# A routed-attention and FFT-gate kernel: one more group's softmax sums go through accumulating DMAs, and thirty warm-up products stand where sixteen did

## The chip, the cores and the metric

The kernel runs on one core of a Trainium2 chip. The core has a matrix engine (TensorE, "PE" in the profile), a vector engine (VectorE, "DVE"), a scalar engine (ScalarE, "ACT"), a general engine (GpSimd, "POOL") and a queue engine (SyncE, "SP") that issues most DMAs. Each takes its instructions strictly in the order in which the program gives them, and they wait for one another on semaphores. The metric is the device time of one execution in microseconds. Three executions of the kernel before took 366.21, 366.43 and 366.46 us; the median is 366.43.

## The reference

Two stages follow each other. The first is attention in which a query sees only the keys of its own cluster; the second is a gated long convolution along the sequence.

```
# attention: q, k, v of 4 batches x 8 heads x 768 positions x 64
q_assign = argmax(normalised q . normalised centroids)      # 16 clusters a head
k_assign = argmax(normalised k . normalised centroids)
scores   = where(q_assign == k_assign, (q @ k.T) / 8, -1e9)
attn     = exp(scores - max) / (sum over keys + 1e-9)
x        = attn @ v                                         # heads put side by side: 4 x 768 x 512
# gate
x1, x2, x3 = split(x @ w_proj)                              # each 768 x 512
x2_conv  = irfft(rfft(x2) * rfft(filter))                   # circular convolution over 768
out      = (x1 * x2_conv * x3) @ w_out
```

## The kernel before

**How the work is cut.** The eight "groups" n = 0 to 7 are half a batch each: four heads, taken as two pairs pr = 0 and 1. For each pair `attention(n, pr)` runs over six blocks of 128 keys (sk = 0 to 5). A block has three score products of 512 columns (L67 or L69 by the array's mode), three exponentials on ScalarE (L647, L650) into one of five buffers `p`, and the products with the values (L661, eight instructions) that add into one pair of PSUM banks. The mask costs no pass of its own: `routing(n)` finds the clusters, and the one-hot rows are written below q and k in the tiles `aug`, so that the score product itself adds a large negative number. `routing` also transposes the loaded q and k of the next groups on TensorE (L551, L562), copies them out of PSUM to `qkP` and casts them into `aug` (L246 on ScalarE, L248 elsewhere). `hyena(b)` is the gate for batch b, after groups 2b and 2b+1; its products (L798, L69) fill TensorE between those of attention.

**The sum of the exponentials.** The denominator of the softmax is a sum over all keys. The blocks are first added to one another into `acc` (two tiles, one for each pr): the first two blocks by three instructions of 512 columns on VectorE or GpSimd (L678, `part`), the other four by one VectorE instruction each (L682). What is left is a sum over the 128 partitions, and it is done in two ways.

- "Late" pairs (groups 0, 1 and 7): `den` multiplies `acc` by a tile of ones on TensorE (L695), `total` copies the result out of PSUM on ScalarE or VectorE (L701, L703), and a small DMA through DRAM (`dd`, 6 KB, L707 and L709) turns it into `dn`. The very last pair (`last`) has a way of its own with more products and no DMA.
- The other pairs (groups 2 to 6): three accumulating DMAs issued by GpSimd (L715) fold the upper half of `acc` on the lower, 64, then 32, then 16 rows; SyncE writes the 16 rows left to DRAM (`dd`, 96 KB, L719) and reads them back so that each partition holds what it must add (`dp`, L721); VectorE adds sixteen rows (`gather`, L725 and L726).

Both then take the reciprocal (L728), send it out and back over all partitions (`dr`, `rb`, L729 and L732), and VectorE multiplies the attention's output with it into `xT` (L761), which `hyena` reads. The same `acc` tile is taken again by the same pr of the next group: its first `part` has to wait until the sum before has been read.

**What sets the order.** `build` first lists every piece of work with the engines that could do it. The constant `ORDER`, a long string, then says the rest: each word is an engine letter and a number (`P1015:3` is piece 1015 on TensorE with PSUM bank 3), in the order in which the pieces are issued. `Plan.follow` reads it. Nothing is scheduled at run time. Which engine casts a tile, which PSUM bank a product takes and how far exponentials run ahead are all fixed there.

**Idle products.** `hot()` fills a tile with ones (L1012) and multiplies it with itself `HOT` times (L1015); nobody reads the results. In the kernel before the tile is the first 640 columns of `y`, into which the filter is loaded later. Of its sixteen products fifteen stand ahead of all other work of TensorE and one among the first transposes.

**The head.** Before the first score product TensorE transposes the first q and k (L562), multiplies them with the centroids (`first_masks`, L497) and VectorE turns that into one-hot rows (L501 to L518), which go into `aug` (L526, L248). GpSimd clears a number of tiles (`constants`), one of them `cbd` (L983).

Of the kernel before, what the change touches and what calls it, by code (L numbers as in the profile page):

```python
# [34 lines left out]
FIRST = 2  # L35
# [4 lines left out]
HOT = 16  # L40
# [84 lines left out]
A35 V0 G18 S45 A46 P14:0 G29 S47 V22 P6:1 G20 S48 P5:2 G28 P11:3 S52 P1:4 G23 P2:5 V36 V53 S51 P16:6 G34 V37 P13:7 V59  # L125
G17 S49 V38 P4:0 V54 A39 A40 P7:1 V60 G19 V55 S50 P10:2 P3:3 G24 V61 P15:4 P9:5 P12:6 G137 V21 V56 P68:7 A66 A63 P70:0
V62 A57 P8:1 G33 S121 V41 A69 P74:2 G27 A58 P76:3 A64 G30 S124 A71 V26 P42:4 A77 V75 G65 S123 G72 P140:5 A67 P142:6
V43 P146:1 V143 S122 P82:7 G25 V141 G32 V44 S120 A73 P80:0 V83 G31 S135 A79 P102:3 V81 G78 P144:2 S134 P138:6 A103 V84
P96:5 A145 G136 S130 P100:4 V85 A97 P94:7 A101 V86 S131 P108:0 A95 G133 V87 A105 S127 P106:3 V88 A139 S126 V89 G104
P149:2 A99 P249:5 S128 G132 P251:4 A151 V93 V91 A250 V90 P243:7 A252 V92 S125 P183:6 V109 P245:5 A244 G98 V107 A184  # L130
S129 P185:0 P187:7 V150 G253 A186 P190:3 S288 V110 P192:6 P194:2 A188 V147 P200:0 V111 S287 A195 P202:7 V112 A246
P204:2 V199 A191 P189:45 V113 A193 V197 A201 A203 V198 P208:3 P210:6 A205 P212:0 V114 P216:7 P196 A211 V207 A209 A213
P218:2 P220:6 A254 P224:3 V148 P226:0 G154 V115 P206 A217 A219 V119 A118 P228:1 V153 P263:7 A116 V155 P214 V117 A221
V215 A248 P293:2 P222 A227 A294 V157 A229 P255:6 V223 A225 P257:0 P295:2 A264 P297:1 P300:3 A258 P261:7 A256 P302:0
V158 P230 A298 V160 A301 A262 V231 A296 P304:6 P310:1 S352 P312:3 A305 P267:72 S291 A303 V156 A232 S292 V159 A311
P233:6 S285 V269 A259 G162 P314:0 V268 S290 P318:1 A313 P299:45 V270 A315 G161 S289 A266 V234 P320:2 S286 P322:7 A319
V271 G152 P163:3 A323 S242 P171:0 A260 P164:6 S235 V272 P326:1 V273 G307 P328:7 A165 P306 A327 V166 A167 G358 P330:1
V274 A169 P316 G353 A331 V275 G309 A329 P334:3 P172:1 A321 V168 S278 P336:7 A175 G356 P177:2 V276 S280 V170 P324 A335
G308 S277 A173 V176 S279 V174 P419:361 S236 G247 A337 A181 V317 G357 A265 P338:0 P178:7 S453 A339 P332 S454 A421 V420
A422 V325 P359:0 A179 P361:1 P363:3 P340 A362 A360 V182 G426 A364 P366:6 V237 P368:1 A342 V180 P370:0 S238 G355 P376:3  # L140
P378:7 A371 V333 P365:45 S282 G354 A369 S455 A367 P380:2 A379 S283 P384:0 V374 P386:1 A381 P388:6 S281 P392:7 V341
A377 P372 S284 A387 S239 A385 P394:2 A389 S240 V375 P396:3 P343:1 A397 V373 A395 P427:063 V383 A393 A344 S345 P400:2
P402:7 A429 P404:1 V391 P382 A430 A428 A401 P461:0 A405 V399 P463:3 P465:6 A403 P390 A466 S346 A425 V407 P468:2
P435:17 S456 A464 V241 P470:6 P472:3 P398 A471 V437 A462 G476 V436 A473 P478:6 V438 P480:0 P482:1 P486:7 A481 P488:3
V347 P406 V439 A469 S348 A433 S458 V440 A483 P409:0 S418 V441 G475 A408 S459 P490:2 A489 P494:1 P467:45 V442 S460 A495
A487 S349 V443 G477 A410 P474 A479 A491 S446 V444 P496:3 S411 V485 P498:1 P502:7 A497 P701:062 S448 A434 S445 A424
V431 S447 P484 A499 V493 S350 S452 P504:3 P506:1 S457 P492 A505 V423 A704 S412 V501 A503 S520 P500 A507 S449 A703 S451
P639:3 V509 P508 A640 S738 A702 P641:7 V413 P643:1 A510 G708 P511:3 S414 A642 G432 P646:0 A644 V512 P648:2 P650:6 A647
G706 P656:7 S513 P658:1 A649 P660:3 P645:45 S450 V351 A657 A661 V653 A651 S416 P664:0 P666:2 A659 P668:7 V655 S415
P672:3 P674:6 A669 P676:1 V707 P652 A673 S514 V654 A677 A665 V663 P709:731 A675 A667 P680:0 V671 P682:6 S741 P684:2  # L150
A681 P662 A685 A711 V515 A683 V679 P743:0 S516 P670 A710 S740 A744 A712 S735 P745:2 V417 P747:6 P750:0 P752:1 P717:37
V687 A753 A746 S518 A748 S517 P754:1 A714 V718 P760:2 G689 P678 S736 V719 A755 G758 V720 S700 A751 P686 V721 P762:6
P764:3 A688 V722 P768:7 P770:1 P772:0 A761 V723 G757 P749:45 A765 A769 V724 P776:2 A771 P778:3 P780:7 P756 A779 V759
A763 V519 A705 G690 P766 V725 A781 V726 P521:1 S728 V767 S804 P523:3 A522 S729 A777 P531:6 S727 V525 A773 S732 V524
P526:7 A532 S730 V775 G691 P784:1 S739 P786:2 P528:0 A787 S742 A527 P533:3 A713 S734 V529 P788:6 P564:2 S733 V534 A789
S737 P774 V535 A785 G537 A715 V530 S692 A565 P805:7 V536 P807:6 P809:1 P812:3 A808 V539 P814:0 P816:2 A810 P782 V783
A806 A815 P822:6 A817 P824:1 P826:7 V538 A823 P830:0 P790 A813 V791 A831 A827 P540:2 S866 A792 P543:6 G819 V542 S693
P867:307 A825 V541 S731 V544 G821 P811:45 A869 V545 A870 V546 G793 A868 P548:1 V547 A873 P832:2 P834:6 V549 G716
P551:0 A833 P838:3 V550 P818 A835 G820 V552 A839 V553 P840:7 P842:2 V829 P875:163 A843 P556:0 V554 A877 S906 P828 A841
V837 A876 G794 A878 P846:2 P566:7 A847 V557 G555 P848:1 P850:3 V694 P909:6 P559:2 A910 P836 V695 V560 A851 S696 A871  # L160
V558 S903 G562 P911:6 V567 P568:3 S907 A912 V561 P913:0 P883:76 A569 G795 V845 S908 A879 S904 A849 P570:2 A914 S698
V884 G563 V885 P916:3 P918:1 P579:0 V886 A919 P920:6 P926:7 A580 P928:1 V887 A917 P844 A921 V853 A929 S796 P572:03
A927 P852 A573 V888 G855 V574 P930:6 G872 V575 P934:1 P581:7 A931 V889 A854 G576 S797 P936:0 P583:3 V582 A882 S901
P938:6 V890 P915:45 A584 A937 V891 G923 A939 P942:7 P922 A880 V571 S896 V577 A943 S894 V925 A874 P587:30 S697 V892
P585:6 V578 G856 S895 A588 A935 P932 S893 V586 G924 A881 S902 V589 V590 P944:2 S899 P946:7 V798 P950:1 P952:6 A947
S905 P594:0 V933 P596:3 A595 A951 P940 A953 V799 V941 S800 G857 A945 P954:7 S970 P1089:0 P598:1 A955 S898 A1090 V699
P1091:6 P1093:2 P1096:7 P1098:0 P948 V949 A1099 A1092 S801 A1097 P1100:0 S802 P1106:6 A1094 P956 V957 S858 A1107 A1101
P1108:7 P600:2 A958 V592 G959 P1110:6 V591 A1109 P1114:0 P1095:45 A599 G593 A1111 V601 V597 S859 P1116:7 P1118:1
P1151:623 A1117 G1105 A1115 A1119 P609:7 A1152 V1154 S1186 P602:01 A1153 V1103 S1187 P1159:236 V1104 A603 S897 A1158
V605 G1155 S900 V604 P1102 A1161 V1113 G960 S1191 A1162 S1190 A1160 P1122:0 P1124:1 A1123 P1167:23 S1192 V803 A610  # L170
G607 P1126:6 V1168 P1112 A1127 G606 V860 A1125 V1169 A1156 P1130:0 G961 P1132:7 V861 V1170 P1134:6 S862 A1131 P1193:1
P1195:2 P1197:3 P1120 A1196 V1121 A1135 A1198 P1200:0 A1133 P1202:2 V1171 P1204:6 P1210:3 A1194 P1212:7 P1128 A1203
S864 V1172 A1201 S1188 V1129 A1211 P611:1 S962 A1163 P1214:2 S863 P1218:0 A1166 P1220:3 V612 P1136 S1185 V1173 A1213
A1205 V1137 P1222:1 A1215 P613:7 A1138 P617:62 S963 A1221 P1199:45 V608 A618 S1189 A614 V1174 P1226:3 P1228:7 P1206
A1227 V620 G1208 A1223 V1175 A1219 P1230:3 V619 A1229 P1216 G1139 S1178 V1176 A1231 G622 S1177 A1157 V964 P1234:1
S1183 P615:0 A1164 V965 G621 P1224 S966 V616 S1180 V1207 S1179 P1236:2 V1209 P1232 A1237 V865 A1235 A1165 P1238:6 V623
P1325:730 S967 A1239 V1217 S968 G1140 P1317:216 S1150 A1328 S1182 A1326 V1225 A1327 S1254 P1240 A1320 S1184 A1319
S1181 A1318 P1255:0 V1233 P1257:3 P1259:7 A1256 P626:1 A1260 A1258 P624:2 P1262:6 V969 G1141 P631:0 A625 A627 V1241
P1264:7 P629:3 A1265 A1263 P981:2 V630 G1243 P971:1 V1321 P973:7 G1324 A972 S1142 A982 P983:6 G1323 V975 A1242 S628
V974 P976:3 A632 V984 P978:1 A977 V985 P1266:2 P1272:7 V979 P1014:0 A1267 S1143 V980 P1274:3 P1276:6 S1352 V987  # L180
P1280:2 A1275 P1261:45 G1244 A1273 V986 S1358 A1281 V988 A1015 S1356 P1282:1 P1284:3 V989 P990:7 A1283 S1351 P1288:2
# [47 lines left out]
def build(T):  # L229
# [25 lines left out]
    def ap(h):  # L255
        return bank(h.ids[0])
# [359 lines left out]
    def attention(n, pr, sins):  # L616
# [8 lines left out]
        for sk in range(NT):  # L625
# [568 lines left out]
```

## Time and profile before

| | us |
|---|---|
| median of three executions | 366.43 |
| the profiled execution | 366.52 |
| its span, first to last instruction | 364.7 |
| TensorE busy in it | 353.9 (97%) |
| VectorE busy | 339.3 (93%) |
| ScalarE busy | 271.1 (74%) |
| GpSimd busy | 137.1 (38%) |
| first score product starts at | 18.35 |
| first product of hyena(0) starts at | 107.19 |

The profile is of one execution. "Busy" is the time in which an engine had at least one instruction under way. The view of groups has a line for each place in the code and shape, with how often it ran, its total time and its mean in nanoseconds; behind the second bar stands the idle time before it and who ended that. The view of the chain follows the work that ended last back to the start: each row has a start, a length and what it was. The timeline lists instructions in order of time, and its brackets hold the idle time before a row and what ended it. The view of stretches gives the busy time of each engine in a window, the granted clock of TensorE as a share of full speed, and the DMA engines' share and rate.

### The profile page before, as it was taken

What the parts mean: (1) busy time and instruction counts of PE and PEld (TensorE: products, weight loads), DVE (VectorE), ACT (ScalarE), POOL (GpSimd) and SP (SyncE); (2) the same over time, 40 slices, a digit from 0 to 9 for tenths busy, and PEclk for the clock granted to TensorE, in tenths of its full rate; (3) what the DMA queues carried; (4) which work ended last, traced back from release to release, by engine and by line L of the source; (5) the groups of instructions that cost most, each with busy time, mean ns of one, the idle gap of its engine ahead of it and who ended that gap; (6) DMA issues with size and microseconds to landing.
All of it is one profiled execution on the core that took longest, in us unless ns stands there. A gap on an engine that the chain in (4) does not pass through costs nothing.

```text
span 364.7 us, 8483 instructions
## 1 busy us (share of the span) xinstructions
PE 353.9 (97%) x3254; PEld 198.8 (55%) x3254; DVE 339.3 (93%) x470; ACT 271.1 (74%) x502; POOL 137.1 (38%) x167
## 2 busy tenths in 40 slices
PE   8799999999999999999999999999999999999994
PEld 4445445454555555665565555555655556475771
DVE  8899889998999999989987999999999999999992
ACT  5999989789878777898987667789969826532232
POOL 8930841122131644344143463432340363045500
PEclk9999999999999999999999999999999999999998
DMA  9990999165576568678667948375755640410214
GB/s 171 226 248 14 218 180 179 26 166 132 120 134 147 102 108 129 130 148 151 131 125 193 174 111 155 43 156 56 178 80 155 89 61 17 162 43 2 117 59 173
DMA packets 88004, 45.69 MB, mean 125 GB/s; under 512 B 76488, under 2 KB 82012, under 8 KB 87964
## 3 DMA queue, kind: packets, MB, share of 16 engines
q1 hardware_dynamic: 84076, 35.16, 40.9%
q0 software_dynamic: 2960, 9.77, 18.6%
q8 instruction: 25, 0.41, 0.5%
q10 hardware_dynamic: 928, 0.23, 0.3%
q14 instruction: 15, 0.12, 0.1%
HBM read 31.59 MB, written 7.40 MB: 107 GB/s over the span
## 4 chain that ended last, share of the span: by engine, by line
PE 77%; DVE 9%; ACT 8%; DMA 3%; issue 2%; SPq 0%; DVEq 0%
PE bank L69 33%; PE pair L661 26%; PE bank L798 6%; PE bank L551 4%; ACT p L650 3%; DVE acc L682 3%; PE bank L583 2%; DMA dn<-dd 2%; PE bank L1015 2%; ACT aug L246 2%; ACT p L647 2%; PE bank L67 2%; DMA aug<-ohT 1%; PE bank L695 1%; PE bank L470 1%
## 5 line engine op out<-in xcount | busy, mean ns | idle before, releaser
L661 PE MATMUL pair<-p,vraw 128*64 128x385 f32 x768 | 140.4, 488 | 0.0
L650 ACT ACTIVATE p<-bank 128x512 f32<-128x512 f32 x192 | 108.5, 614 | 18.0 <-PE bank L69 15.6
L682 DVE TENSOR_TENSOR acc<-p,acc 128x1536 f32<-128x1536 f32 x64 | 112.1, 1751 | 2.1
L661 PEld LDWEIGHTS pair<-p,vraw 128*64 128x64 f32 x768 | 54.5, 136 | 47.6 <-issue 38.8
L69 PE MATMUL bank<-aug,aug 80*64 80x256 bf16 (+3 forms) x708 | 78.9, 327 | 1.3 <-DMA aug<-ohT 0.7
L647 ACT ACTIVATE p<-bank 128x512 f32<-128x512 f32 x96 | 57.8, 613 | 16.8 <-PE bank L69 11.3
L69 PEld LDWEIGHTS <-aug 80*64 80x64 bf16 (+1 forms) x708 | 40.9, 109 | 42.4 <-issue 29.7
L715 POOL DMA_DIRECT2D acc<-acc x30 | 24.1, 805 | 75.1 <-DMA acc<-acc 30.6
L678 POOL TENSOR_TENSOR acc<-p,p 128x512 f32<-128x512 f32 x23 | 29.8, 1298 | 48.6 <-ACT p L650 13.6
L69 PE MATMUL bank<-xT,wpj 128*64 128x384 bf16 x480 | 46.3, 326 | 0.0
L69 PEld LDWEIGHTS <-wpj 128*64 128x64 bf16 x480 | 27.6, 110 | 15.8 <-issue 5.3
L246 ACT CAST aug<-qkP 64x768 bf16<-64x768 f32 x43 | 35.4, 829 | 0.7
L246 ACT COPY qkP<-bank 128x512 f32<-128x512 f32 (+1 forms) x56 | 28.4, 562 | 7.9 <-PE bank L69 5.8
L69 PEld LDWEIGHTS <-y 128*64 128x64 bf16 x480 | 23.8, 110 | 11.5 <-issue 2.4
L822 DVE TENSOR_TENSOR tm<-bank,hm 128x512 f32<-128x512 f32 x44 | 27.9, 682 | 0.9 <-POOL y L826 0.2
L826 POOL TENSOR_TENSOR y<-tm 128x512 bf16<-128x512 f32 x17 | 21.5, 1275 | 13.9 <-DVE tm L822 8.7
L69 PE MATMUL bank<-wout,y 128*64 128x512 bf16 x192 | 23.1, 379 | 0.0
L798 PE MATMUL bank<-wpj,xT 128*64 128x512 bf16 x192 | 21.9, 379 | 0.0
L248 POOL CAST aug<-qkP 64x768 bf16<-64x768 f32 x17 | 13.9, 827 | 20.5 <-DVE dn L728 8.3
L246 ACT COPY ob<-bank 128x512 f32<-128x512 f32 x21 | 12.2, 594 | 11.0 <-PE bank L69 9.3
L900 POOL TENSOR_TENSOR y<-yy,x 128x768 bf16<-128x768 f32 x7 | 13.1, 1868 | 18.7 <-DVE yy L897 13.8
L551 PE MATMUL bank<-ident,qkraw 128*128 128x128 f32 x144 | 18.1, 276 | 0.0
(161 smaller groups left out, 447.2 us busy)
## 6 DMA issues: line engine op xcount, KB each, us to landing
qkraw<-in_k_dram SPq DMA_DIRECT2D x32, 192.0 KB
vraw<-in_v_dram SPq DMA_DIRECT2D x16, 384.0 KB
qkraw<-in_q_dram SPq DMA_DIRECT2D x31, 192.0 KB
rb<-dr SPq DMA_DIRECT2D x30, 192.0 KB
out_dram<-ob SPq DMA_DIRECT2D x11, 512.0 KB
acc<-acc POOLq DMA_DIRECT2D x10, 384.0 KB, 5.0
acc<-acc POOLq DMA_DIRECT2D x10, 192.0 KB, 3.9
wpj<-in_moe_w_proj_dram POOLq DMA_DIRECT2D x4, 384.0 KB, 6.3
```

What stands on the lines that cost most here:

```text
L69: T.nc.tensor.matmul(out[64 * i:64 * i + 64], lhsT[:, 64 * i:64 * i + 64], rhs, start=start, stop=stop)
L246: T.nc.scalar.copy(out, in_)
L551: T.nc.tensor.transpose(bank(h.ids[i // 4])[:, block(i % 4, 2 < i < NT)], raw(ss[i // NT], i % NT), T.ident)
L647: T.nc.scalar.activation(o, ap(h).rearrange("p (a b) -> p a b", a=2), Act.Exp, scale=0.125)
L650: T.nc.scalar.activation(flat(s)[:, lo:lo + 512], ap(h), Act.Exp, scale=0.125)
L661: T.nc.tensor.matmul(o[64 * hp:64 * hp + 64, ch, :385], T.vraw[vs][:, hp, sk * D:(sk + 1) * D], T.p[slots[sk]][:, hp, 384 * ch:384 * ch + ...
L678: alu(e).tensor_tensor(o, x, y, op=Alu.add)
L682: T.nc.vector.tensor_tensor(T.acc[os], T.p[slots[sk]][:, :, :S], T.acc[os], op=Alu.add)
L715: op(("POOL", .8), lambda e, rows=rows: T.nc.gpsimd.dma_start(flat_()[:rows], flat_()[rows:2 * rows], accum_op=Alu.add), te, r=[], w=AK, b ...
L798: T.nc.tensor.matmul(ap(h)[64 * i:64 * i + 64], T.xT[xs][:, kt, tokens(m, i, w_)], T.wpj[:, kt, DM:2 * DM], start=kt == 0, stop=kt == ND - 1)
L822: op(("DVE", .68), lambda e, i=i, cs=cs, r=r, h=h: T.nc.vector.tensor_tensor(T.tm[r][:, cs], ap(h), hmrow(i, (0, 2, 2, 3)[2 * r + cs]), op ...
L826: op({"POOL": 1.3, "DVE": .68}, lambda e, i=i, r=r: alu(e).tensor_tensor(T.y[:, i, r], T.tm[r][:, 0], T.tm[r][:, 1], op=Alu.add if r else ...
```

## The change

`FIRST` goes from 2 to 1, so that the two pairs of group 1 leave the "late" way and take the accumulating DMAs; `LATE = 14` and `spread` say for the last group what was said before in other words (pairs 14 and 15 are group 7, and `spread` holds for the last pair alone, as `last` did). `HOT` goes from 16 to 30, and the products get a tile of their own, 512 columns wide, of which the first 128 serve as weights. `ORDER` is another string throughout.

In the new order twenty idle products stand ahead of all other work of TensorE, eight more among the transposes and centroid products before the first score product, and two behind it. Beside the pieces that the first paragraph names, some pieces stay what they are and change their engine: of the 48 `part` instructions 33 run on VectorE where 25 did, and 15 on GpSimd where 23 did; ScalarE gets three more casts to `aug` (46 for 43), two more copies to `qkP` and two loads of q and k to issue, and gives three copies of the output to VectorE. The first product of hyena(0) stood in TensorE's order between the value products of group 2's two pairs; it now stands behind the first score product of group 3's second pair. One load of `w_proj` now stands in GpSimd's queue behind the third accumulating DMA of group 2's first pair. In the head GpSimd clears `cbd` as one of its first pieces, where it did so behind other clears and a cast.

```diff
-FIRST = 2
+FIRST, LATE = 1, 14
-HOT = 16
+HOT = 30
...
 ORDER = """
-A35 V0 G18 S45 A46 P14:0 G29 S47 V22 P6:1 G20 S48 P5:2 G28 P11:3 S52 P1:4 G23 P2:5 V36 V53 S51 P16:6 G34 V37 P13:7 V59
...
-        late = n == NG - 1 or n < FIRST
+        late = n < FIRST or 2 * n + pr >= LATE
+        spread = last and late
         if late:
             h, den_, dk = Bank(), lambda: T.den, ["den"]
...
-        if not last:
+        if not spread:
             if late:
...
     def hot():
-        op(("DVE", .6), lambda e: T.nc.vector.memset(T.y[:].rearrange("p i r d -> p (i r d)")[:, :640], 1.0), 0, w=["hot"])
+        op(("DVE", .5), lambda e: T.nc.vector.memset(T.hot, 1.0), 0, w=["hot"])
         for i in range(HOT):
             h = Bank("head")
             op(("PE", .215), lambda e, h=h: T.nc.tensor.matmul(
-                ap(h), T.y[:].rearrange("p i r d -> p (i r d)")[:, 512:640], T.y[:, 0, 0], start=True, stop=True), .1 * i,
+                ap(h), T.hot[:, :128], T.hot, start=True, stop=True), .1 * i,
                r=["hot"], w=[h], alloc=h, free=[h])
...
+    T.hot = tl([128, 512], BF16, "hot")
```

More of the change, by code (lines that the diff above doesn't have):

```diff
@@ L130 @@
[L130 to L139, printed above, removed]
@@ new lines @@
+S876 V611 P1132:2 S1204 P629:3 A1133 V621 P1120 A1174 G1176 S1205 V623 A1129 S1203 V622 A899 P1134:2 P1136:0 V628
+P1140:1 P1142:6 A1137 V821 P1130 A1141 A1143 V624 P1177:701 A1135 V630 V1122 A1173 V1123 P1144:6 P1138 G978 A1179
+S1208 V1121 A1145 V1131 S1168 A1180 P1148:3 S1209 P1150:2 P1152:6 P1146 A1151 S877 V1139 A1153 A1178 P1211:2 A1149
+P1213:6 P1215:0 P1218:1 A1184 S1207 P1185:73 V1147 A1212 G979 A1219 P631:2 A1214 V1186 G625 A1216 V1187 P1220:1
+P1222:6 P1228:0 A1221 V1188 G1181 P1230:3 P1232:7 P1236:1 P1154 A1233 V1189 A1223 A1237 V1155 P1238:7 P1240:6 A1156
@@ L226 @@
+V1926 P1950:0 V1931 P1946:1 P1947 P1951 P1932:4 V1948 P1933 V1952 S1949 P1936 P1939:7 A1934 S1953 A1937 P1940 P1942:3
+V1941 S1938 P1943 V1944 S1945
 """
@@ L759, in attention @@
         xv = lambda: T.xT[xs][:, kt].rearrange("p (a b) -> p a b", a=2)
-        for a_ in [slice(0, 2)] if not last else [slice(0, 1), slice(1, 2)]:
-            op(("DVE", .6 if last else 1.01), lambda e, a_=a_: T.nc.vector.scalar_tensor_tensor(
-                xv()[:, a_], osv()[:, a_], eps(), ap(rk[a_.start])[:, :384].unsqueeze(1) if last else rbv(), op0=Alu.add,
-                op1=Alu.mult), te + (4 if last else 12), r=[("osb", o3)] + (rk[a_] if last else rk), w=[("xT", xs, kt)],
-               free=rk[a_] if last else [], lock=True)
+        for a_ in [slice(0, 2)] if not spread else [slice(0, 1), slice(1, 2)]:
+            op(("DVE", .6 if spread else 1.01), lambda e, a_=a_: T.nc.vector.scalar_tensor_tensor(
+                xv()[:, a_], osv()[:, a_], eps(), ap(rk[a_.start])[:, :384].unsqueeze(1) if spread else rbv(), op0=Alu.add,
+                op1=Alu.mult), te + (4 if spread else 12), r=[("osb", o3)] + (rk[a_] if spread else rk), w=[("xT", xs, kt)],
+               free=rk[a_] if spread else [], lock=True)
     INV = [("inv", j) for j in range(4)] + [("inv", j, i) for j in (4, 5) for i in range(2)]
```

185 lines of the change are left out of this document (95 added, 90 removed).

## The prediction

> **What bounds the kernel now.** I read the stretches first, then the chain, then the groups. The page gives one busy line for the span:
>
> ```profile
> span 364.7 us, 8483 instructions
> PE 353.9 (97%) x3254; PEld 198.8 (55%) x3254; DVE 339.3 (93%) x470; ACT 271.1 (74%) x502; POOL 137.1 (38%) x167
> ```
>
> An average of 97% and 93% leaves open which of the two is the bound. The stretches say it (window, length, then PE, PEld, DVE, ACT, POOL with counts, granted clock, DMA share, GB/s):
>
> ```profile
> 0.00:20.00 20.00, 16.40 (x108) 8.65 (x109) 17.03 (x47) 15.82 (x31) 17.62 (x49) 1.00 1.01 199
> 20.00:60.00 40.00, 39.02 (x296) 19.35 (x294) 37.27 (x49) 38.36 (x71) 15.34 (x23) 1.00 0.80 160
> 60.00:120.00 60.00, 59.90 (x500) 30.47 (x500) 57.30 (x60) 51.16 (x97) 12.55 (x12) 1.00 0.54 125
> 120.00:200.00 80.00, 79.91 (x738) 46.31 (x736) 74.89 (x98) 65.83 (x120) 33.92 (x34) 1.00 0.72 138
> 200.00:320.00 120.00, 119.35 (x1137) 67.50 (x1134) 116.62 (x157) 86.62 (x162) 43.62 (x40) 1.00 0.57 111
> 320.00:357.00 37.00, 37.00 (x472) 25.52 (x471) 34.82 (x62) 11.15 (x23) 14.09 (x10) 1.00 0.13 50
> ```
>
> From 60 us on TensorE is idle for 0.10, 0.09, 0.65 and 0 us: there the length is the sum of its instructions, and what is added to or taken from them counts in full. VectorE has 2.73 + 2.70 + 5.11 + 3.38 + 2.18 = 16.1 us of slack after 20 us, thinly spread. From 20 to 60 us three engines are nearly full together: ScalarE has 40 - 38.36 = 1.64 us left, TensorE 0.98. Ahead of 20 us it is a matter of waits. These are the rows of the head and of VectorE in it:
>
> ```profile
> 1.58 5.68 PE L1015 MATMUL bank<-y 128*128 128x512 bf16 x13 [1.58 <-DVE y L1012]
> 1.58 6.11 PE L1015 MATMUL bank<-y 128*128 128x512 bf16 x15 [1.58 <-DVE y L1012]
> 7.54 0.82 PE L562 MATMUL bank<-ident,qkraw 128*128 128x128 f32 x6
> 9.17 0.67 PE L397 MATMUL bank<-identb,fw 128*128 128x128 bf16 x4
> 10.01 1.84 PE L497 MATMUL bank<-qkP,cb 128*32 128x384 f32 x16
> 14.57 1.62 PE L497 MATMUL bank<-qkP,cb 128*32 128x384 f32 x16 [1.03 <-ACT qkP L246]
> 18.35 0.38 PE L67 MATMUL bank<-aug,aug 80*128 80x512 bf16 x1 [0.79 <-DVE aug L248]
> 11.35 0.22 DVE L324 COPY cbd<-bank 64x64 f32<-64x64 f32 x1 [1.05 <-POOL cbd L983]
> 11.83 1.05 DVE L501 STREAM_TRANSPOSE sim<-bank 128x384 f32<-128x384 f32 x2
> ```
>
> Thirteen idle products take 5.68 us (about 0.43 each), the next two add 0.43 together, 0.22 each. The rate doubles at about 7.1 us, and nothing later falls back: every stretch reads a clock of 1.00, though TensorE stood still for 1.03 and 0.79 us.
>
> **Part 1, group 1's sums leave TensorE.** The chain of waits holds the products that go, one row for each pair (start, length):
>
> ```profile
> 72.57 0.78 PE bank L695 x8
> 85.05 0.78 PE bank L695 x8
> ```
>
> They stand where TensorE has no idle time, so two of them are worth -1.56 us. What a pair takes instead, and the neighbours of it, by the groups and the DMA issues:
>
> ```profile
> L701 ACT ACTIVATE den<-bank 128x384 f32<-128x384 f32 x4 | 2.0, 498 | 2.0 <-PE bank L695 2.0
> L725 DVE TENSOR_REDUCE dn<-dp 128x12 f32<-128x192 f32 x10 | 4.8, 482 | 0.0
> L726 DVE TENSOR_SCALAR dn<-dn 128x12 f32<-128x12 f32 x10 | 3.4, 339 | 0.3
> L715 POOL DMA_DIRECT2D acc<-acc x30 | 24.1, 805 | 75.1 <-DMA acc<-acc 30.6
> acc<-acc POOLq DMA_DIRECT2D x10, 384.0 KB, 5.0
> acc<-acc POOLq DMA_DIRECT2D x10, 192.0 KB, 3.9
> acc<-acc POOLq DMA_DIRECT2D x10, 96.0 KB, 3.7
> ```
>
> For two pairs: VectorE +2 x (0.48 + 0.34) = +1.6 us; GpSimd +6 issues x 0.8 = +4.8 us, beside 62% idle time; ScalarE one copy of `den` less (-0.50). SyncE loses two writes and two reads of 6 KB and gets two writes and two reads of 96 KB. In its queue the write for pair (1,0) waits for the third fold, and three mask writes for pair (2,1) stand behind it; by my count of the work ahead these are wanted some 10 us later, so I cost them at nothing; if that cover is gone, each microsecond of it goes to the first score of (2,1).
>
> The sum's consumer has to wait longer. Pair (3,1) shows the new way:
>
> ```profile
> 159.54 0.82 POOL L715 DMA_DIRECT2D acc<-acc  x1 [7.00 <-DVE acc L682]
> 182.72 0.49 DVE L725 TENSOR_REDUCE dn<-dp 128x12 f32<-128x192 f32 x1
> 193.72 1.01 DVE L761 SCALAR_TENSOR_TENSOR xT<-osb,rb 128x768 bf16<-128x768 f32 x1
> 82.99 1.76 DVE L682 TENSOR_TENSOR acc<-p,acc 128x1536 f32<-128x1536 f32 x1
> 105.55 1.00 DVE L761 SCALAR_TENSOR_TENSOR xT<-osb,rb 128x768 bf16<-128x768 f32 x1
> 107.19 3.62 PE L798 MATMUL bank<-wpj,xT 128*64 128x512 bf16 x32
> ```
>
> From the first fold to the first of the folded sum's instructions on VectorE it is 182.72 - 159.54 = 23.2 us, and 34.2 us to the product with `rb`. With a den product the same distance was 105.55 - 84.75 = 20.8 us (from the end of the pair's last addition, 82.99 + 1.76). So the first product of `hyena(0)`, which began 1.6 us behind that row, cannot stand at 107 any more: 34 us behind 84.75 and the same 1.6 give about 120, and the changed order puts it there, behind the first score product of group 3's second pair. No instruction is added by that, but between the two pairs of group 2 TensorE now has attention alone to do, and so has no filler when an exponential is late. From the durations of the pieces I count 12.75 us of VectorE against 12.09 us of TensorE for that pair, so VectorE sets the pace there by 0.66 us, less what runs ahead. I take +0.4 us, with 0 and +0.66 as bounds.
>
> **Part 2, sums of two blocks move to VectorE.** The rows of both engines, and those of ScalarE that part 3 uses:
>
> ```profile
> L678 DVE TENSOR_TENSOR acc<-p,p 128x512 f32<-128x512 f32 x25 | 17.3, 717 | 0.2 <-ACT p L650 0.2
> L678 POOL TENSOR_TENSOR acc<-p,p 128x512 f32<-128x512 f32 x23 | 29.8, 1298 | 48.6 <-ACT p L650 13.6
> L650 ACT ACTIVATE p<-bank 128x512 f32<-128x512 f32 x192 | 108.5, 614 | 18.0 <-PE bank L69 15.6
> L246 ACT CAST aug<-qkP 64x768 bf16<-64x768 f32 x43 | 35.4, 829 | 0.7
> L246 ACT COPY qkP<-bank 128x512 f32<-128x512 f32 x34 | 18.3, 604 | 1.6 <-PE bank L551 1.5
> L442 ACT ACTIVATE tm<-bank,hw 128x512 f32<-128x512 f32 x7 | 4.8, 699 | 1.4 <-DVE hm L446 1.4
> ```
>
> Eight `part` instructions cost VectorE 8 x 17.3/25 = +5.5 us and save GpSimd 8 x 1.3 = 10.4 us that nobody lacks. The remaining changes of side (three output copies come, some copies, casts and gate products go) cancel to within a microsecond or two. With part 1 VectorE gets some 5 to 7 us more, against 16.1 us of slack. Bounds: 0 if the slack lies where the work comes, 7 if it doesn't. I put nothing on it beyond the 0.4 above, since the slack is over twice the load in every long stretch; the upper end is a rival below.
>
> **Part 3, ScalarE early.** By the two orders, ScalarE has up to the end of group 1's first pair three casts more (3 x 0.83), a copy to `qkP` (0.60) and an exponential (0.61), and less by a copy of mask rows (0.83, as long as a cast) and one `den` (0.50): +2.4 us, and it issues two loads more, for which I add 0.3 in all: 2.7. It has 1.64 us idle between 20 and 60 us. If all of this is usable, 1.1 us remain; if ScalarE's waits for VectorE's filter products (1.4 of the 1.64, L442 in that stretch) stay as they are, 2.4 remain; and if TensorE or VectorE hold the end of the stretch anyway, nothing. I take +1.5, between the first two and nearer the first, because any shift opens some of those waits; bounds 0 and 2.7.
>
> **Part 4, fourteen more idle products.** Five more ahead of the transposes: at the rate behind 7.1 us 5 x 0.216 = 1.08 us, less 0.1 for the shorter clearing of the tile, so the first transposes start at about 8.5 in place of 7.54. Eight lie among pieces with waits of 1.03 and 0.79 us and cost 8 x 0.216 = 1.7 us at most. Against this stands `cbd`: VectorE waited 1.05 us for it at 11.35, and that wait goes. The first eight centroid products took half of 1.84 us from 10.01 on, so their result stood at about 10.95 and `sim` at 11.83 had 0.9 us of slack, made by `cbd`. The delay of 0.98 eats this slack and 0.1 more; four more of the filter's transposes (L397, 0.17 each, and L400, under 0.1 each) stand ahead of the centroid products, some 0.3 beyond what `fw` made TensorE wait for. So the first score product comes 0.4 us later, at 18.75; bounds -0.8 (the slack all gained) and +1.5 (nothing of it). The two idle products behind the first score, 0.43 us, stand where ScalarE's exponentials lead the chain: I take half, 0.2; bounds 0 and 0.43.
>
> The granted clock is 1.00 from 7.1 us on, through gaps of 1.03 us. The Trainium skill, "TensorE: Matmul & The Clock Gate", Part 1 ("The HAM clock gate"), says that the clock is held at half until the array was busy for a window of about 3.4 us, counted in time and not in products, and that it falls back after an idle window of that length. The trace agrees as to the start (the rate doubles after 5.5 us of products), and the gaps here are under a third of such a window, so by this rule the products placed in gaps protect nothing that the profile shows; where they would, the sum would gain what is priced as the last rival below.
>
> **The sum.** -1.56 (den products) + 0.4 (no filler in group 2) + 1.5 (ScalarE early) + 0.4 (head) + 0.2 (idle products behind the score) = +0.94 us. The profiled execution took 366.52 us, 1.8 of it around its span, and is 0.09 above the median of 366.43. 366.52 + 0.94 = 367.46; against the median 367.4.
>
> **Rivals.**
> - Faster. The order is another one throughout, and each of my positive terms is a wait that it may cover: with ScalarE's 2.7 hidden and the filler not missed, -1.56 + 0.2 + 0.4 = -1.0 gives 365.4; with the head's slack gained as well (-0.8 in place of +0.4), 364.3. For it: every product that goes stood in a full stretch. Against: 20 to 60 us is full on three engines, and what is added lies there.
> - VectorE becomes the bound behind group 1: then its 5 us stand in place of the 0.4 and hide ScalarE's. -1.56 + 0.6 + 5 = +4.0, 370.4; with 5.4 instead 370.8. It decides where VectorE's idle time in 60 to 120 us (2.70) is used up. Against: TensorE's own idle time there is 0.10.
> - The `acc` tile comes free too late. The tile of pair (1,1) can be taken by pair (2,1) only when the third fold was read:
>
> ```profile
> 100.09 1.29 POOL L678 TENSOR_TENSOR acc<-p,p 128x512 f32<-128x512 f32 x1
> 178.28 0.37 SPq L721 DMA_DIRECT2D dp<-dd  x1
> ```
>
> By these rows the first sum of (2,1) stood 100.09 - 84.75 = 15.3 us behind the last addition of (1,1), and a folded pair holds its tile for up to 178.28 - 159.54 = 18.7 us from the first fold. 3.3 us of wait, passed on by five buffers `p` that fill: less the den products and with the head, 366.4 - 1.56 + 0.6 + 3.3 = 368.8. It decides if fold and write take over 15 us; two folds of 5.0 and 3.9 us and a third of 3.7 leave them at 13 when GpSimd isn't late.
> - No change: the -1.56 is eaten by waits just so, 366.4.
> - The idle products save a clock that falls in executions without a profile: a fall between 14 and 19 us would cost up to 2 us. Three times within 0.25 us of each other speak against; I count it with "faster", for 0.02.
>
> **How the numbers follow.** A measurement of this kernel can tell about 0.2%, 0.73 us, from no change. My forecast (366.7 to 368.6, by the bounds of its own terms) gets 0.42, of which 0.06 lies within 0.73; VectorE as bound 0.08; the late tile 0.08; faster 0.32; no change 0.10. Slower: 0.36 + 0.08 + 0.08 = 0.52; same 0.06 + 0.10 = 0.16; faster 0.32. The range goes from the fastest of "faster", 364.3, to the upper price of VectorE, 370.8; outside it lie combinations of late tile and full VectorE, and gains of which I see no source.
>
> **What would show it.** Right: no L695 for two pairs, TensorE still idle under 0.3 us between 60 and 120 us; ScalarE's share of 20 to 60 us up to 39 us or more, and the end of group 1's first pair about 1 to 2 us later; first score product at about 18.7; the first product of `hyena(0)` near 120. Wrong on ScalarE: the first value products of group 1 at the same time as before. Late tile: a wait of (2,1)'s first `part` for the write of `dd`, and TensorE idle near 100 us. VectorE: TensorE idle by several microseconds in short waits for `p` behind 75 us. The forecast fails on the other side if the first score product comes before 18 us.

## The result and the profile after

The changed kernel takes 370.79 us (median of six executions, 368.95 to 372.11), the kernel before 366.36 (six beside it). The ratio is 1.0114, with a 95% interval of 1.0096 to 1.0132: the change makes the kernel slower by 4.4 us. The time lies in the predicted range (364.3 to 370.8) by its last hundredth; the forecast was 367.4. The executions also scatter more than those of before, over 3.2 us in place of 0.4 (over 1.4 in nineteen later executions of the kernel before).

The profiled execution took 369.83 us, about 1 us less than the median, with a span of 368.0. Its stretches (window, length, PE, PEld, DVE, ACT, POOL with counts, clock, DMA share, GB/s) and the first row of its list of TensorE's waits:

```profile
20.00:60.00 40.00, 38.36 (x285) 19.01 (x285) 37.77 (x48) 38.36 (x73) 17.53 (x23) 1.00 0.83 166
60.00:120.00 60.00, 57.65 (x465) 30.27 (x463) 56.68 (x61) 53.56 (x99) 14.51 (x17) 1.00 0.75 140
120.00:200.00 80.00, 78.38 (x734) 46.71 (x732) 76.90 (x102) 59.60 (x111) 32.52 (x31) 1.00 0.69 131
200.00:320.00 120.00, 120.00 (x1125) 70.16 (x1123) 115.59 (x156) 89.35 (x164) 42.60 (x39) 1.00 0.60 121
...
PE bank L69 <- DMA aug<-ohT: 4.2, 3, 2.0
```

TensorE's idle time between 60 and 120 us rose from 0.10 to 2.35 us, and between 120 and 200 us from 0.09 to 1.62. Its waits for the DMAs that write the mask rows into `aug` rose from 0.7 us to 4.2: 0.89 us at the first score product of group 1, 2.02 at that of group 3, 1.31 at the second of group 5. VectorE is no fuller than before between 60 and 120 us (56.68 against 57.30 us). The longest of the three, in the timelines of TensorE, SyncE and GpSimd, and GpSimd's loads of `w_proj` in the list of DMA issues (count, size, us to landing):

```profile
111.04 1.46 PE L662 MATMUL pair<-p,vraw 128*64 128x385 f32 x8
114.53 1.06 PE L69 MATMUL bank<-aug,aug 80*64 80x512 bf16 x10 [2.02 <-DMA aug<-ohT]
...
104.89 1.44 SPq L723 DMA_DIRECT2D dp<-dd  x1
106.42 4.04 SPq L483 DMA_DIRECT2D aug<-ohT  x4
...
108.31 0.76 POOL L717 DMA_DIRECT2D acc<-acc  x1 [3.79 <-DMA acc<-acc]
108.81 0.83 POOL L1007 DMA_DIRECT2D wpj<-in_moe_w_proj_dram  x1
...
wpj<-in_moe_w_proj_dram POOLq DMA_DIRECT2D x4, 384.0 KB, 6.0
```

The four writes for pair (3,0) leave SyncE by 110.46 us and are waited for until 114.53. In the middle of them GpSimd issues a quarter of `w_proj`, which takes about 6 us to land. The kernel before issued all four quarters by 56 us. Its own rows for (3,0) left no earlier: the last of the four writes is the fourth of the first row here, and the second row begins with the first score product of group 3.

```profile
108.81 2.44 SPq L482 DMA_DIRECT2D aug<-ohT  x4
114.97 1.48 PE L69 MATMUL bank<-aug,aug 80*64 80x512 bf16 x16
```

That write left at 111.25 us, and TensorE came to the product at 114.97 without a wait. In the changed kernel TensorE was there at 114.53 - 2.02 = 112.51 us, since products of `hyena(0)` no longer stand in front. The head, with ScalarE's first exponential of both kernels (the first row is of the kernel before):

```profile
18.80 0.63 ACT L650 ACTIVATE p<-bank 128x512 f32<-128x512 f32 x1
```

```profile
1.46 7.25 PE L1017 MATMUL bank<-hot 128*128 128x512 bf16 x20 [1.46 <-DVE hot L1014]
8.55 0.82 PE L563 MATMUL bank<-ident,qkraw 128*128 128x128 f32 x6
18.87 0.38 PE L67 MATMUL bank<-aug,aug 80*128 80x512 bf16 x1
20.25 0.64 ACT L651 ACTIVATE p<-bank 128x512 f32<-128x512 f32 x1
```

The first score product comes 0.52 us later, the first exponential 1.45 us.

### The profile page after: what moved, and what is told of

Its sections match the earlier page's. It is cut to its first block, busy times and chain, and to the rows that moved or that the text cites. A ratio compares the mean times of both kernels' runs of the same rounds, so it can differ in the third digit from the quotient of the medians.

```text
span 368.0 us, 8530 instructions
## 1 busy us (share of the span) xinstructions
PE 355.2 (96%) x3253; PEld 205.9 (56%) x3256; DVE 344.6 (94%) x479; ACT 271.8 (74%) x504; POOL 134.3 (36%) x164
## 4 chain that ended last, share of the span: by engine, by line
PE 72%; DVE 11%; DMA 8%; ACT 5%; issue 2%; SPq 1%; POOL 0%; DVEq 0%; POOLq 0%; ACTq 0%
PE bank L69 32%; PE pair L662 23%; PE bank L800 6%; DVE acc L683 4%; DMA aug<-ohT 3%; DMA acc<-acc 3%; PE bank L552 2%; PE bank L1017 2%; PE bank L584 2%; PE bank L67 2%; DMA dp<-dd 1%; ACT qkP L247 1%; DVE acc L679 1%; ACT p L651 1%; PE bank L471 1%
## 5 line engine op out<-in xcount | busy, mean ns | idle before, releaser
L69 PE MATMUL bank<-aug,aug 80*64 80x512 bf16 (+3 forms) x692 | 77.9, 327 | 5.1 <-DMA aug<-ohT 4.2
L717 POOL DMA_DIRECT2D acc<-acc x36 | 28.7, 797 | 104.6 <-DMA acc<-acc 47.4
L69 PE MATMUL bank<-xT,wpj 128*64 128x384 bf16 x496 | 48.0, 326 | 0.2 <-ACT p L648 0.2
L247 ACT CAST aug<-qkP 64x768 bf16<-64x768 f32 x46 | 37.9, 830 | 1.9 <-PE bank L69 1.1
L69 PEld LDWEIGHTS <-wpj 128*64 128x64 bf16 x496 | 30.9, 110 | 14.4 <-issue 5.6
L247 ACT COPY qkP<-bank 128x512 f32<-128x512 f32 (+1 forms) x59 | 30.3, 563 | 8.4 <-PE bank L69 5.9
L69 PEld LDWEIGHTS <-y 128*64 128x64 bf16 x496 | 26.0, 110 | 10.9 <-issue 2.5
L679 POOL TENSOR_TENSOR acc<-p,p 128x512 f32<-128x512 f32 x15 | 19.2, 1278 | 24.1 <-ACT p L648 11.5
L679 DVE TENSOR_TENSOR acc<-p,p 128x512 f32<-128x512 f32 x33 | 21.7, 689 | 1.5 <-DMA dd<-acc 1.1
L552 PEld LDWEIGHTS bank<-ident,qkraw 128*128 128x128 f32 x144 | 15.5, 141 | 4.7 <-ACT p L651 1.9
```

The costliest lines, as they stand in the source:

```text
L69: T.nc.tensor.matmul(out[64 * i:64 * i + 64], lhsT[:, 64 * i:64 * i + 64], rhs, start=start, stop=stop)
L247: T.nc.scalar.copy(out, in_)
L552: T.nc.tensor.transpose(bank(h.ids[i // 4])[:, block(i % 4, 2 < i < NT)], raw(ss[i // NT], i % NT), T.ident)
L679: alu(e).tensor_tensor(o, x, y, op=Alu.add)
L717: op(("POOL", .8), lambda e, rows=rows: T.nc.gpsimd.dma_start(flat_()[:rows], flat_()[rows:2 * rows], accum_op=Alu.add), te, r=[], w=AK, b ...
```

## The experiments

The first theory was that TensorE loses its time to mask rows that land late, because of where SyncE and VectorE have them in their queues. The rivals were VectorE as the bound, the idle products, and the accumulating DMAs as such. Times are to be held against 370.8 (changed) and 366.4 (before).

**1. Nobody waits for the rows.**

```diff
+UNREAD = [(3, 0), (5, 0)]
...
+                        T.junk[64 - 64 * hp + 16 * j:80 - 64 * hp + 16 * j] if (n, pr) in UNREAD else
                         T.augs[a][hp][j][64 - 64 * hp:80 - 64 * hp], T.ohT[rows]), due + .3 * hp,
```

> The changed kernel, but the eight mask writes for the first pairs of groups 3 and 5 go to a tile that nobody reads, so their score products do not wait for these rows (they use the rows of an earlier group: the mask of those two pairs is not this group's). VectorE, the DMAs and every queue do what they did. Theory 'mask rows': TensorE loses its 2.3 us ahead of group 3 and 1.5 us ahead of group 5 to nothing but these writes landing late; without them 3.8 us go: from 370.8 to about 367.0, and the spread between executions (369 to 372) shrinks to under 1 us, since the time to landing is what varies. Rival 'VectorE is the bound': the wait only moves, TensorE then waits for exponentials or sums behind it: less than 1 us gained, 370 or more. Rival 'idle products': no change.

Measured 367.05 us (ten executions, 364.94 to 370.08): 3.7 us gone with all of VectorE's work and all DMAs in place. VectorE isn't the bound; the waits are the loss. In its profile TensorE still waits 1.7 us for other mask rows (0.78 at group 1, 0.92 at 122.36 us). The spread did not shrink, so something else varies as well.

**2. The rows leave earlier, by order alone.**

```diff
-... V743 ... V775 S531 ... V776 ... V777 ... V744 ... S748 ... S746 ... S747 ... S745 ...
+... V743 V744 ... V775 ... V776 ... V777 ... S748 ... S746 ... S747 ... S745 S531 ...
-... S882 S881 S1196 S1198 S1195 S1197 ...
+... S1196 S1198 S1195 S1197 S882 S881 ...
```

(V744 and its like are L609; S531 reads `dp`, S745 to S748 and S1195 to S1198 write mask rows, S881 and S882 write `rb`.)

> The changed kernel with words of the order moved and no work changed: on VectorE the last one-hot instruction (L609) of groups 1, 3 and 5 stands right behind the transpose L607 (in group 3 it stood behind three sums of 1.85 us together, in group 5 behind 2.1 us of other work); on SyncE the read of dp for pair (1,1) stands behind the four mask writes for (3,0), and the two rb writes behind those for (5,0). Theory 'mask rows', with the place in the queues as the cause: the rows of group 3 land 1.1 to 1.8 us earlier, those of group 5 1.5 us or more, TensorE's waits fall from 4.2 us to 1.5 or less: 367.8 to 369. Rival 'VectorE is the bound': it does the same work, so within 0.5 us of 370.8. Rival 'idle products': no change.

Measured 370.76 us: no gain. The waits ahead of groups 3 and 5 were gone, but others stood in their place. One was again for mask rows, directly ahead of the first product of `hyena(0)`, where the second pair of group 3 begins. Behind the moved `rb`, `xT` came late, then a copy of `ob` on VectorE, and TensorE stood still for 1.81 us:

```profile
122.73 0.63 PE L69 MATMUL bank<-aug,aug 80*64 80x512 bf16 x6 [1.56 <-DMA aug<-ohT]
...
203.01 0.62 PE L69 MATMUL bank<-aug,aug 128*64 128x512 bf16 x4 [1.81 <-DVE ob L249]
203.44 2.33 PE L662 MATMUL pair<-p,vraw 128*64 128x385 f32 x8
```

The stretches around the second show what happened next (granted clock third from the right):

```profile
202.00:203.00 1.00, 0.00 (x0) 0.00 (x0) 1.00 (x3) 0.52 (x1) 0.09 (x1) 1.00 1.00 331
203.00:204.00 1.00, 0.99 (x8) 0.64 (x9) 1.00 (x2) 0.55 (x2) 0.73 (x1) 0.97 1.00 385
204.00:205.00 1.00, 1.00 (x6) 0.43 (x4) 1.00 (x3) 1.00 (x3) 0.00 (x0) 0.50 1.42 293
205.00:206.00 1.00, 1.00 (x8) 0.40 (x6) 0.90 (x3) 0.02 (x1) 0.00 (x0) 0.50 0.92 164
206.00:207.00 1.00, 1.00 (x8) 0.61 (x6) 1.00 (x1) 0.00 (x0) 0.00 (x0) 0.50 0.97 168
207.00:208.00 1.00, 1.00 (x13) 0.65 (x11) 0.55 (x1) 0.49 (x2) 0.00 (x0) 0.82 1.26 90
```

The clock went to half for about 3.4 us, by my estimate at a cost of some 1.7 us: the wait was paid twice. The products bear the clock out: eight value products took 2.33 us, where the same eight took 1.46 in the changed kernel's timeline.

**3. The same without moving `rb`.** The `rb` writes stay; two mask writes of (3,1) go ahead of the read of `dp` as well.

```diff
-... V743 ... V775 S531 ... V776 ... V777 ... V744 ... S748 ... S745 ... S534 ... S751 ... S752 ...
+... V743 V744 ... V775 ... V776 ... V777 ... S748 ... S745 S751 S752 S531 ... S534 ...
```

> The changed kernel with the order mended without the two rb writes being moved: L609 behind L607 in groups 1, 3 and 5 on VectorE; on SyncE the four mask writes of (3,0) and two of (3,1) ahead of the read of dp for pair (1,1). In the run before, the waits for the mask rows ahead of groups 3 and 5 were gone, but TensorE waited 1.81 us at 201 us for a copy of ob on VectorE, which stood behind xT and so behind the rb writes that had been moved back, and behind that wait its granted clock was 0.58 for 4 us. Theory 'mask rows': without that new wait 2 to 3.5 us go: 367.3 to 368.8. Rival 'VectorE is the bound': another wait takes the place again, 370 or more.

Measured 371.24 us, and a new wait again, in the lists of TensorE's waits and in VectorE's and SyncE's timelines:

```profile
PE pair L662 <- ACT osb L686: 3.3, 1, 3.3
...
116.24 0.48 DVE L727 TENSOR_REDUCE dn<-dp 128x12 f32<-128x192 f32 x1 [5.58 <-DMA dp<-dd]
...
109.56 0.58 SPq L723 DMA_DIRECT2D dp<-dd  x1
```

Now the read of `dp` was the one that left at 109.6 to 110.1 us, and VectorE's wait for it ended at 116.24, 6.7 us after the issue began; the median of such reads in this run's list of DMA issues, counted the same way, is 4.0. VectorE stood behind it for 5.58 us, the copy to `osb` behind VectorE, TensorE behind the copy. In the changed kernel it was the mask rows; here it was `dp`: whatever SyncE issues at that time lands late. Both show in the same window, and that is where the load of `w_proj` runs.

**4. Without the idle products, in the changed and in the mended order.** The fourteen additional products are not issued; the second run has the order of experiment 3 in addition.

```diff
+SKIP = {1, 2, 3, 5, 10, 16, 18, 19, 22, 23, 24, 25, 26, 29}
-            op(("PE", .215), lambda e, h=h: T.nc.tensor.matmul(
+            op(("PE", .215), lambda e, h=h, i=i: None if i in SKIP else T.nc.tensor.matmul(
```

> The changed kernel with the fourteen additional idle products not issued: fifteen stand ahead of the transposes and one among them, as before. Theory 'mask rows': the head alone changes; transposes start 1.1 us earlier, the first score product 0.5 to 1.0 us earlier, all behind it moves along, but the waits ahead of groups 3 and 5 stay: 369.8 to 370.4. Rival 'idle products': they are what made the kernel slower: 14 x 0.216 = 3.0 us go, 367.8. If they hold up the clock in executions without a profile, it becomes slower than 371.

> The same order as the run above and, in addition, without the fourteen additional idle products. If the waits for mask rows and the idle products ahead of the head are separate losses, both go: 1.4 to 1.7 us for the head from what the run above gives, 365.6 to 367.0, and it is at or under the kernel before (366.4). If they are two names of one loss (a later head that only shifts into a wait), no better than the better of the two alone, 367.4.

Measured 367.46 us (366.31 to 370.53) and 370.03 us. The head of the first:

```profile
7.17 0.82 PE L564 MATMUL bank<-ident,qkraw 128*128 128x128 f32 x6
17.12 0.38 PE L68 MATMUL bank<-aug,aug 80*128 80x512 bf16 x1
18.85 0.64 ACT L652 ACTIVATE p<-bank 128x512 f32<-128x512 f32 x1
```

The five products in front cost 8.55 - 7.17 = 1.38 us, and the first exponential moves by 20.25 - 18.85 = 1.40: nothing behind them absorbs any of it. That is more than the 1.08 us of five products at the full rate; the rest, 0.3 us, is by my estimate from the two starts that in the changed kernel's profile one to two products more ran at 0.43 us before the rate doubled. The remaining gain of the median is not the head's: in the profiles the wait ahead of group 3 stayed (2.32 us), and the one in group 5 (1.31 us) was not there. The second run has the same wait for `osb` as experiment 3, 3.4 us.

**5. Idle products in the wait itself.**

```diff
-SKIP = {1, 2, 3, 5, 10, 16, 18, 19, 22, 23, 24, 25, 26, 29}
+SKIP = {24, 25, 26, 29}
-... S751 P823:0 ...
+... S751 P2:1 P3:3 P4:1 P6:3 P11:1 P17:3 P19:1 P20:3 P23:1 P24:3 P823:0 ...
```

> The changed kernel without the additional idle products in the head, ten of them placed instead directly ahead of the first score product of group 3, where TensorE waits 2.3 us for mask rows (10 x 0.216 = 2.2 us, so they end about when the rows land). Its twin without them gave 367.46 (366.31 to 370.53 in ten executions), the slow ones with a lower mean granted clock (0.993 and 0.994). Theory 'a wait of about 2 us lets the clock fall in some executions': TensorE is busy in the wait, the clock stays, no execution over 368, median 366.5 to 367.2. Rival 'the spread is that of the landing of the rows alone': same median and spread as the twin, or up to 0.5 us more where the rows land early.

Measured 368.09 us (eight executions, 367.64 to 370.77), not under its twin's 367.46. None of them had a mean clock under 0.997, where three of the twin's ten had 0.993 or 0.994 and took 369.2 to 370.5. That fits products that hold the clock, but does not show it: none in eight against three in ten can be chance, and the kernel before has an execution with 0.995 that took 366.25 us. What it shows is that executions of over 370 us occur with a clock of 0.998 and 1.000 too, so the clock isn't the whole of the spread. That the landing of the rows is the rest is not shown; none of the long executions was profiled.

**6. Group 1's sums back on TensorE, with and without the idle products.**

```diff
-        late = n < FIRST or 2 * n + pr >= LATE
+        late = n <= FIRST or 2 * n + pr >= LATE
...
-... G423 ... P420 A441 ... G424 ... G527 ... P678:6 ... G528
+... P423:0 P420 A441 A424 ... P678:6 P527:7 V528 ...
```

> The changed kernel with the sums of group 1 taken back to TensorE: eight den products for each of its two pairs, copies of den, small DMAs; no accumulating DMAs for them; everything else stays in its place in the queues (the later first product of hyena(0) too). Theory 'mask rows': TensorE gets 1.56 us more; VectorE is freed of two gathers (1.5 us) and of 1.1 us of waiting for the acc tile, SyncE of the long reads of dp, so the rows of group 3 land about 1.8 us earlier: 370 to 371. Rival 'the accumulating DMAs themselves are the loss': back to the time of before and 1 us of slack: under 368.5. Rival 'den products were pure cost': 372.3.

> The changed kernel with both named parts undone: group 1's sums on TensorE again, and no additional idle products. What is left is the new order with its moved pieces. If the parts add up, 368.6 less 1.4 to 3.3 us: 365.3 to 367.2. If the new order by itself is worse than that of before, over 367.2.

Measured 368.61 and 368.50 us. By the first the accumulating DMAs look like a loss of 2.2 us; by the second, with both named parts undone, the order alone is still 2.1 us behind the kernel before. In the profile of the first TensorE waits for no mask rows behind 60 us; in that of the second (370.36) two waits of 1.33 us each stood at 124 and 197 us. The parts do not add up: without the idle products it is 367.46 us, without the fold 368.61, without both 368.50.

**7. The load of `w_proj` alone.** One word of the order moves.

```diff
-... G387 A393 ... A807 G369 V532 ...
+... G387 G369 A393 ... A807 V532 ...
```

> The changed kernel with one word moved: the load of the second quarter of w_proj, which GpSimd issues at 108.8 us in the changed order (all four were issued by 56 us before), goes to 61 us, into GpSimd's idle time. The prediction did not price it. Theory 'the load meets the mask rows': the four writes for (3,0) were issued by 110.5 us and landed at 114.5, 4.1 us later, where those for (5,0) took 2.6; without the load they land 1.0 to 1.7 us earlier and TensorE's 2.3 us ahead of group 3 shrink by as much, and where the wait stays under 2 us the clock does not fall in other executions either: 368.3 to 369.8. Rival 'SyncE's queue and VectorE alone set the landing': no change, 370.3 to 371.3.

Measured 367.24 us (ten executions, 366.38 to 367.45; ratio to before 1.0016, 1.0007 to 1.0025). One DMA issued at 61.3 in place of 108.8 us takes 3.5 us off, where 2.5 was expected at best, and the spread falls from 3.2 to 1.1 us. Between the two profiles the gain is 2.4 us; the rest is in executions that were not profiled. The changed kernel's stretches around group 3's start, and then those of this run:

```profile
108.00:110.00 2.00, 2.00 (x15) 0.89 (x14) 1.90 (x2) 1.37 (x4) 1.33 (x2) 1.00 1.05 96
110.00:112.00 2.00, 2.00 (x14) 0.86 (x12) 1.93 (x5) 1.52 (x3) 0.02 (x1) 1.00 0.70 64
112.00:114.00 2.00, 0.51 (x4) 0.00 (x0) 2.00 (x3) 0.00 (x0) 0.81 (x1) 1.00 0.96 187
114.00:116.00 2.00, 1.47 (x14) 0.90 (x16) 1.90 (x2) 1.03 (x3) 0.00 (x0) 1.00 0.47 76
```

```profile
108.00:110.00 2.00, 2.00 (x15) 0.82 (x14) 1.90 (x2) 1.76 (x4) 0.68 (x1) 1.00 0.61 67
110.00:112.00 2.00, 2.00 (x16) 0.97 (x14) 1.93 (x5) 1.56 (x3) 0.24 (x1) 1.00 0.14 41
112.00:114.00 2.00, 2.00 (x20) 1.02 (x18) 2.00 (x2) 0.80 (x2) 0.58 (x1) 1.00 0.09 15
114.00:116.00 2.00, 2.00 (x22) 1.07 (x18) 1.90 (x2) 2.00 (x5) 0.00 (x0) 1.00 0.59 132
...
60.00:120.00 60.00, 59.89 (x485) 31.62 (x483) 57.16 (x62) 55.44 (x103) 14.38 (x17) 1.00 0.73 143
```

With the load gone the DMA engines are nearly idle from 110 to 114 us (0.14 and 0.09), the rows of (3,0) arrive in time, and TensorE is full. SyncE's and VectorE's queues are word for word those of the changed kernel, so their places in the queues are not enough to make the rows late: it takes the load in flight. The place matters only as it decides what meets the load (in experiment 2 the rows left by 106.7 us, ahead of it, and were not late at group 3). Which resource the load and the small writes share is not shown.

**8. What the rest of the change is worth.** The early load, no additional idle products, and L609 early on VectorE only; and the same with group 1 on TensorE.

```diff
+SKIP = {1, 2, 3, 5, 10, 16, 18, 19, 22, 23, 24, 25, 26, 29}
...
-... V289 ... V290 ... G387 A393 ... V743 ... V744 ... G369 V532 ... V1193 ... V1194 ...
+... V289 V290 ... G387 G369 A393 ... V743 V744 ... V532 ... V1193 V1194 ...
```

> The load moved as above, no additional idle products, and on VectorE alone L609 directly behind L607 in groups 1, 3 and 5; SyncE's queue stays that of the changed kernel. From 367.5 (without the idle products): the load is worth 1.0 to 1.7 us and L609 up to 1 us more, if the rows of group 3 are what TensorE waits for: 364.8 to 366.3, under the kernel before. If neither load nor L609 is the cause, 367.0 to 367.8; if freeing one wait opens the next, as in the two runs with SyncE's queue changed, over 368.

> The kernel of 365.2 us (changed kernel, early load of w_proj, no additional idle products, L609 early) with group 1's sums taken back to TensorE: sixteen den products more, four gather instructions on VectorE and six accumulating DMAs less. This prices part 1 of the change by itself. By the prediction's terms the den products cost 1.56 us where TensorE has no idle time, and taking them back frees VectorE of 1.5 us that was hidden: 366.4 to 366.9. Rival 'the fold costs as much as it saves' (its waits ahead of group 3 and the late hyena): 365.0 to 365.6. Rival 'the fold was a loss', as the run with den products (368.6 against 370.8) looked: under 364.8.

Measured 365.16 us (twelve executions, 364.67 to 366.39) and 366.92 us (eleven, 366.54 to 368.46). The first is faster than the kernel before: ratio 0.9969, 0.9959 to 0.9979. The second is 1.76 us slower than the first, which is the price of two times eight den products (1.56) and a little more. The fold of group 1 is a gain of that size once the load is out of its way. From experiment 7 to the first run here it is 2.1 us for the idle products and L609 together; they were not parted. Its profile still has a wait of 0.78 us for mask rows ahead of group 3 (at 111.48 us), so late rows are fewer, not gone.

**9. The kernel before with its own mask rows earlier.**

```diff
-... V1341 V1374 S1346 V1249 S1344 V1342
+... V1341 V1342 V1374 S1346 V1249 S1344
```

> The kernel before with one instruction moved: L608 of group 6 on VectorE directly behind the transpose L606, ahead of a sum (0.68 us) and a reciprocal (0.22 us). Its one wait for mask rows was 0.93 us, ahead of group 6. Theory 'mask rows': half of the rows leave 0.75 us earlier, the wait falls by 0.4 to 0.75 us: 365.6 to 366.0. Rival 'the rows' landing is set by SyncE and the DMA engines': 366.3, no change.

Measured 366.92 us (ratio 1.0014, 1.0005 to 1.0022): slightly slower, not faster. SyncE's four writes took until 237.5 us, 0.2 us earlier than before, and group 6 began at 239.60 in place of 239.49. (The wait there is 0.65 us in the profile before, not the 0.93 of the expectation.) In the new profile no wait is left there, but the value products just ahead took 2.11 us in place of 1.57, so nothing was gained. The place of L608 on VectorE isn't what sets the landing there, so in experiment 8 the share of L609 in the gain is open too; it was not run by itself.

## Why the prediction was right and wrong

The sign was right; the forecast was 3.4 us short, and that the time still lies in the range is luck. The upper end, 370.8, is the price of VectorE as the bound, and no run shows that. The sum was +0.94 us; with the one word moved the changed kernel stands at 367.24 against 366.37, +0.87. So a term was missing. That the others sum up so well is luck too, as two of them are off by about 1 us each way (head and ScalarE, below). Of the signs named, TensorE's idle time in 60 to 120 us was to stay under 0.3 us and was 2.35, and ScalarE's share of 20 to 60 us was to reach 39 us and stayed at 38.36.

- **The step that failed** is in part 1: "No instruction is added by that", for the later `hyena(0)`. The section on the change names the load of `w_proj` that goes behind the third fold of group 2's first pair, but no step prices it. Part 1 counted the small transfers that the fold itself adds, and not the largest one, which the new order moves into the same microseconds; the load costs 3.5 us by experiment 7. The sentence on SyncE's queue, which costs the rows of (2,1) at nothing, held: TensorE waits for none of them. The rows that came late were those of (3,0).
- **Den products, -1.56.** Right within the noise: 1.76 by experiment 8.
- **No filler in group 2, +0.4 (bounds 0 and 0.66).** The place was right, the mechanism was not: not VectorE's pace but the mask rows were late there, 2.0 us. In the kernel before, products of `hyena(0)` stood in front, and TensorE came to these rows at 114.97 us; in the changed kernel it came at 112.51. So the later `hyena(0)` did cost a cover, that of the rows. Without the load the place costs nothing (0.11 us idle in 60 to 120 us).
- **Head, +0.4.** The first score product was forecast at 18.75 and came at 18.87, but out of two errors: the idle products in front cost 1.4 us where 1.1 less the slack were put, and without the fourteen the product comes at 17.12, 1.2 us earlier than before. What counts is the first exponential, 1.45 us later, as copies to `qkP` stand ahead of it on ScalarE; without the fourteen it comes at 18.85, where it was before (18.80). So head and idle products, put at 0.6 us together, are 1.4.
- **ScalarE early, +1.5.** Not borne out. Group 1's first score product came at 54.45 in place of 52.44, +2.01, close to the +2.1 that head, ScalarE and idle products were put at together. But without the fourteen idle products it came at 52.97 (experiment 4), so they make 1.48 of it, and 0.53 is left for ScalarE and all else that was moved ahead of that point. The end of group 1's first pair came 1.3 us later, as forecast (73.9 in place of 72.6), but for the same reason: without the idle products it came at 72.5. (ScalarE has three more copies to `qkP`, 59 for 56 in the list of groups, where the section on the change says two.)
- **VectorE as the bound (0.08).** Not so: its work grew by 5.3 us (344.6 us busy), within the 5 to 7 that were counted, but experiment 1 keeps all of it and gains 3.7 us.
- **The `acc` tile late (0.08).** VectorE did wait 1.1 us for it, at pair (2,0) and not (2,1); TensorE did not stand still for that.
- **The idle products and the clock (0.02).** The clock does fall behind a wait (experiment 2), but the products in the head are not what keeps it up: without them the twelve executions of experiment 8's first run had mean clocks of 0.998 to 1.000. That every stretch reads 1.00 says less than the prediction took from it, as the view reads 1.00 also before 7 us, where the idle products took 0.43 us each. The rule drawn on was an idle window of about 3.4 us, as the Trainium skill, "TensorE: Matmul & The Clock Gate", Part 1, has it. The trace of experiment 2 differs: a fall followed a standstill of 1.81 us, and here the measurement decides.
- The first product of `hyena(0)` was put near 120 us and began at 124.1.

## What to carry to other kernels

When an order is rewritten, list every large transfer that changes its time, not only those of the edit, and look what small transfers somebody waits for are on their way in the same microseconds. A small DMA that lands late is found by what it costs, but here it was mended by moving the large one: moving the small ones about took the wait away and opened others that cost as much (experiments 2 and 3). A part that looks like a loss in a kernel with such a collision (the fold, 2.2 us) can be a gain without it (1.8 us), so undo the collision first and price the parts then.

## What the runs showed that was not expected

- With one DMA of 384 KB in flight, a read of `dp` took 6.7 us from issue to landing in place of 4.0 (experiment 3).
- A standstill of TensorE of 1.81 us was followed by about 3.4 us at a granted clock of 0.50, in another run one of 3.32 us by a stretch of 4 us at 0.65:

```profile
116.00:120.00 4.00, 1.00 (x4) 0.43 (x6) 3.69 (x5) 1.85 (x4) 1.65 (x1) 0.92 0.21 28
120.00:124.00 4.00, 4.00 (x24) 1.90 (x22) 3.83 (x5) 2.60 (x5) 0.85 (x1) 0.65 0.65 205
```

  The first of these falls came 0.9 us after TensorE had begun again (203.01 us; half clock from about 203.94 by the stretches). The standstill of 2.02 us in the changed kernel's profile was followed by none, and neither was that of 2.32 us in experiment 4's first run. So the length of a standstill alone does not tell whether the clock falls.
- What remains open: which resource of the DMA engines the load takes from the small writes, how the gain of experiment 8 divides between the idle products and L609, why the wait ahead of group 5 was in some executions and not in others, and how much of the changed kernel's median beyond its profile (1 us) is the clock and how much the landing.
